# An mLSTM cell and a feed-forward block in float32: where the weights of the third chunk are split, which queue stores them, and when the keys of the next chunk but one are loaded

## The chip, the cores and the metric

The kernel runs on one core of a Trainium2 chip. The metric is device time in microseconds (us). Three runs of the kernel before took 465.68, 472.87 and 473.05 us; their median is 472.87. The engines are named as in the profile: PE (matmul; PEld is its weight load), DVE (vector), ACT (scalar), POOL (GpSimd) and SP, which here only issues DMAs. ACT and POOL can issue DMAs too; what an engine's instruction stream holds is done in order, DMA issues included.

## The reference

The inputs are q, k, v and an output gate of shape (4, 8, 768, 40) (batch B, heads H, sequence S, head size D), an input and a forget gate of shape (4, 8, 768), and two weight matrices, 320x2048 and 2048x320, all float32. First an mLSTM cell runs over the sequence:

```
for t in range(S):
    m_new = maximum(f[t] + m, i[t])
    fs, is_ = exp(f[t] + m - m_new), exp(i[t] - m_new)
    m = m_new
    C = fs * C + is_ * outer(v[t], k[t])
    n = fs * n + is_ * k[t]
    y[t] = sigmoid(o[t]) * (C @ q[t]) / maximum(abs(n . q[t]), 1)
```

Then y, as a matrix x of 3072 tokens by 320, goes through a feed-forward block: h = x @ w_in, g = h * sigmoid(1.702 h), out = g @ w_out.

## The kernel before

**Chunks.** The sequence is cut into NW = 6 chunks of 128 steps, w = 0 to 5; a chunk has 4 x 128 = 512 tokens. In the text, the second, third and fourth chunk are w = 1, 2, 3. The attention of a chunk is computed as small matrix products against the 32 (batch, head) pairs, with a state carried from chunk to chunk. The program is written out by hand: the order of the calls in the source is the order on each engine. One turn of the main loop does the feed-forward block of chunk w and, woven into its second half, the attention of chunk w+1.

**Up stage.** `up_fast(w, j)`, j = 0 to 7, computes h for 256 of the 2048 hidden columns: 16 matmuls of 128x128 by 512 columns (L777). Precision comes from splitting: a weight w_in[n] (n = j // 2, 128x2x512) is rounded to `w_high`, and its rest is kept twice, as `w_low` (w_in - w_high) and, in another scaling, as `w_diff`; the activations are split in the same way into x_high, x_low, x_diff and x_rest. Pass j=0 takes the operands in the order high, rest, low, rest, diff, the others rest, diff, high, low. ACT copies the "side" sums out of PSUM (L801), DVE adds the "main" sums (L805), ACT applies the GELU (L754). The banks in PSUM alternate: pass j+2 needs those of pass j to be read out. In chunk w=1, n = 2 and 3 (`LATE`) are not split yet: L782 uses the unsplit weights there.

**Down stage.** `down_fast` gives 14 products (i = 0 to 13) of g with w_out (L868), each 16 instructions in the trace. After product i, `side[i]` runs parts of the attention of chunk w+1: for w+1 = 2 to 5, scaling and weights at i = 0 to 2, `carry` (p_c, with the keys k_st) at 3, `scores` (p_s) at 4, `values` (p_o, p_i) at 5 and 6, the seam at 6, 10 and 11. The seam brings y into the feed-forward layout: stores to DRAM (`seam_out`, L562), loads back into q_sq (`seam_in`, L571), block transposes on DVE (`seam_turn`), and the splits of x (`split_x`, `split_on`).

**Where the splits live.** `split_high` (L688, ACT), `split_diff` (L691, DVE) and `split_low` (L697, POOL or DVE) make the three parts. The tiles share slots in turn: w_high 2 and 3 go to the slots of w_in 1 and 2, so w_high 3 needs w_in 2 to have been read for the last time, by split_diff and split_low of 2. In chunk w=2, w_low 2 and 3 take the slots of g 2 and g 3 of chunk 1 and w_diff those of its `sums`; g 6 and g 7 of chunk 2 take the slots of w_low 2 and 3 again. w_diff and w_low do not stay in SBUF: `keep` (L701) stores them to DRAM rows (`w_row`, 512 KB each), `fetch_diff` (L725) and `fetch_low` (L721) load them again for each later chunk, in the down stage ahead of it: w_diff 0 and 1 and w_low 2 at i = 11, w_diff 2 and 3 at i = 13. w_low 3 is loaded once by `keep_last` (L705) to stay.

**Loads.** From w=1 on all loads are issued by SP, in this order around the change. In the up stage of chunk w, for the attention of chunk w+1: the gates' round trip through DRAM (m_row, st_row, raw, wt; L310 to L409) and v_st and k_st (L126). At the end of the up stage the output gate `eo` (L128). In the down stage, the gates fi of chunk w+2 (L98), `load_squares(w+2, "k")` (L114: four DMAs of 320 KB into k_sq, which the next up stage turns into kT from its pass j=3 on) at i = 0, the seam's loads, fetch_diff, fetch_low, the stores of `out` (L877), and `load_squares(w+2, "q")` (into q_sq) at i = 13.

The lines that matter most, of the up stage and the down stage in the main loop of the kernel before:

```
                if w == 2 and j == 1:
                    for n in LATE:
                        split_high(n); split_diff(n); split_low(n, G)
                if w == 2 and j == 3:
                    for n in LATE:
                        keep(w_diff_row, n, w_diff[2, n]); keep(w_low_row, n, w_low[2, n])
                    keep_last()
...
            if w and w + 2 < NW and i == 0:
                load_squares(w + 2, "k")
```

Of the kernel before, what the change touches and what calls it, by code (L numbers as in the profile page):

```python
# [8 lines left out]
FP = mybir.dt.float32  # L9
# [22 lines left out]
def kernel(  # L32
# [12 lines left out]
    nc = tc.nc  # L45
# [4 lines left out]
    NW = S // L  # L50
# [25 lines left out]
    V, A, G, T = nc.vector, nc.scalar, nc.gpsimd, nc.tensor  # L76
# [31 lines left out]
    def load_squares(w, what):  # L108
        for dst, src in [((k_sq, k), (q_sq, q))["kq".index(c)] for c in what]:
            x = src[:, :, w * L:(w + 1) * L, :].rearrange("b (p two) (r c) d -> two r (b p) (c d)", two=2, c=4)  # L110
            for i in range(2):
                for n in range(2):
                    r, at = slice(i * 64 + n * 32, i * 64 + n * 32 + 32), (1 - n) * 32
                    nc.sync.dma_start(out=dst[r, at:at + BH // 2 * 4 * D].rearrange("r (j x) -> r j x", x=4 * D), in_=x[i])  # L114

    def load(w, what, bs=slice(0, B)):
        hs = slice(bs.start * H, bs.stop * H)
        for c in what:
            if c == "o" and w not in eo:
                eo[w] = ld.tile([L, BH, D], FP, tag="eo", bufs=1, name="eo")  # L120
            dst, src = {"k": (k_of(w), k), "q": (q_st, q), "v": (v_st, v), "o": (eo.get(w), o_gate)}[c]
            if w and c in "kv":
                for i, t, r in ((0, slice(0, L), slice(0, L)), (1, slice(0, HL), slice(HL, L)),
                                (1, slice(HL, L), slice(0, HL))):
                    x = src[:, :, w * L + t.start:w * L + t.stop, :].rearrange("b (p two) s d -> two s (b p) d", two=2)
                    nc.sync.dma_start(out=dst[r, i::2, 0:D], in_=x[i])  # L126
                continue
            nc.sync.dma_start(out=dst[:, hs, 0:D],  # L128
                              in_=src[bs, :, w * L:(w + 1) * L, :].rearrange("b h s d -> s (b h) d"))
# [538 lines left out]
    w_high, w_low, w_diff, w_rest = {}, {}, {}, []  # L668
    w_low_row, w_diff_row = {}, {}
    LATE = (2, 3)  # L670
# [15 lines left out]
    def split_high(n):  # L686
        w_high[n] = win.tile([128, 2, 512], FR, tag="wb" if n < 2 else "wa", name="w_high")
        A.activation(out=w_high[n], in_=w_in[n], func=AF.Copy, scale=BIAS)  # L688

    def split_diff(n):  # L690
        V.scalar_tensor_tensor(out=w_diff[2 if n in LATE else 1, n], in0=w_high[n], scalar=-1.0 - 1.0 / BASE,  # L691
                               in1=w_in[n], op0=OP.mult, op1=OP.add)

    def split_low(n, engine):
        if n not in LATE:
            w_low[n] = win.tile([128, 2, 512], FR, tag="wa" if n else "wb", name="w_low")
        engine.tensor_tensor(out=w_low[2, n] if n in LATE else w_low[n], in0=w_in[n], in1=w_high[n], op=OP.subtract)  # L697

    def keep(row, n, x):
        row[n] = rows.tile([128, 1024], FP, tag=f"{'d' if row is w_diff_row else 'l'}{n}", bufs=1, name="w_row")  # L700
        nc.sync.dma_start(out=row[n], in_=x.rearrange("p c m -> p (c m)").bitcast(FP))  # L701

    def keep_last():
        w_low[3] = work.tile([128, 2, 512], FR, tag="wx", bufs=1, name="w_low")
# [10 lines left out]
    def split_rest_low():  # L715
        wr = w_rest[0]
        V.tensor_tensor(out=wr[64:128, 0::2], in0=w_in_x[0:64], in1=wr[0:64, 0::2], op=OP.subtract)
        V.tensor_tensor(out=wr[64:128, 1::2], in0=w_in_x[64:128], in1=wr[64:128, 1::2], op=OP.subtract)
# [169 lines left out]
    def run(calls):  # L888
        for f, *args in calls:
            f(*args)  # L890
# [62 lines left out]
    for w in range(NW):  # L953
        more = w + 1 < NW
        if w == 0:
            for j in range(NF // 2):
                if j % 2 == 0:
                    ahead, behind = converted[j // 2]
                    run([(convert, p) for p in ahead] + [(fetch, p) for p in fetched.get(j // 2, ())])
                    up(w, j, lambda: run([(columns_turn, 1) if p is None else (convert, p) for p in behind]))  # L960
                if j == 6:
                    load(1, "o")
                if j == 1:
                    wait_for(w_in[1][:, 1, :])
                    scale(0, 1)
                    load(1, "v")
                if j < B and j % 2:
                    carry(0, j // 2)
                if j == 3:
                    masks()  # L970
                    gates(1)
                    columns_in(1)
                if j == 4:
                    spread(1)
                    load_squares(1, "q")
                if j >= B:
                    transposes(1, j - B)
        else:
            if w == 1:
                split_diff(1)  # L980
                split_low(1, V)
            for j in range(NF // 2):
                up_fast(w, j)
                if more and j == 0:
                    gates(w + 1)
                    if w == 1:
                        wait_for(ends[w + 1])
                if w == 1 and j < 4:
                    weight_sums(j)
                if w == 1 and j == 1:  # L990
                    for n in (0, 1):
                        keep(w_diff_row, n, w_diff[1, n])
                if w == 2 and j == 1:
                    for n in LATE:
                        split_high(n)
                        split_diff(n)
                        split_low(n, G)
                if w == 2 and j == 3:
                    for n in LATE:
                        keep(w_diff_row, n, w_diff[2, n])  # L1000
                        keep(w_low_row, n, w_low[2, n])
                    keep_last()
                if more and j == 2:
                    columns_in(w + 1)
                    spread(w + 1)
                    load(w + 1, "vk")
                if more and j:
                    for n in ((), (), (0, 2), (4, 6), (1, 3), (5, 7), ())[j - 1]:
                        block_transposes(w + 1, n)
                if more and j == 7:  # L1010
                    columns_turn(w + 1)
                lag = 3 if w == 1 else 2
                if lag <= j < 4 + lag:
                    hidden_difference(w, j - lag)
                if j >= 6:
                    hidden_sums(w, (j - 6,), G)
            gelu_fast(w, NF // 2 - 1, 1)
            if more:
                load(w + 1, "o")
            hidden_sums(w, (2, 3), V)  # L1020
        side = attention(w + 1) if more else {}
        if more:
            rooms(w + 1)
        if w == 0:

            blocks = [(lambda b=b, n=n: down(w, b, n)) for n0 in (0, 2) for b in range(B) for n in (n0, n0 + 1)]
        else:
            blocks = down_fast(w, 0) + down_fast(w, 1)
        for i, block in enumerate(blocks):
            if w == 0 and i in (0, 4, 5):  # L1030
                convert((17, 18, 19)[max(i - 3, 0)])
                if i == 0:
                    for n in (1, 3, 5, 7):
                        block_transposes(1, n)
            if w + 2 < NW and i == (6 if w == 0 else 0):
                load_gates(w + 2)
            if w and w + 2 < NW and i == 0:
                load_squares(w + 2, "k")
            if w == 0 and i == 13:
                load_squares(w + 2, "k")  # L1040
            if w == 0 and i == 15:
                load_squares(w + 2, "q")
            block()
            run(side.get(i, []))
            if w == 0 and i == 5:
                split_high(0)
                split_rest()
                split_high(1)
            if w == 0 and i == 9:
                split_diff(0)  # L1050
                split_low(0, V)
                split_rest_low()
            if w and more:
                if i == 11:
                    fetch_diff(w + 1, (0, 1))
                    if w > 1:
                        fetch_low(w + 1)
                if i == 13:
                    if w > 1:
                        fetch_diff(w + 1, (2, 3))  # L1060
                    if w + 2 < NW:
                        load_squares(w + 2, "q")
# [30 lines left out]
```

## Time and profile before

| | |
|---|---|
| median of three runs | 472.87 us |
| the profiled execution | 470.54 us |
| its span, first to last instruction | 468.8 us |
| mean granted PE clock in the span | 0.988 |
| PE / PEld busy | 452.9 us (97%) / 394.8 us (84%) |
| DVE / ACT / POOL busy | 330.2 (70%) / 213.2 (45%) / 134.6 us (29%) |
| DMA | 65.43 MB, mean 140 GB/s |
| up stages of w = 1, 2, 3, 4, 5 | 30.89, 37.59, 29.40, 29.41, 29.39 us |
| down stages of w = 1, 2, 3, 4, 5 | 42.98, 41.20, 41.90, 39.25, 30.44 us |

The stages are read from the chain that ended last: the up stage from the first p_h product (L777) of a chunk to its first p_out product (L868), the down stage from there to the next chunk's first p_h. The last down stage holds no attention. The work of the up stages of w = 2 to 5 is the same on PE, and so is that of the down stages of w = 1 to 3; the one of w = 4 leaves out one half of `carry`.

How to read the rows: a row of the chain or the timeline begins with the start and the length in us; then come the engine, the program's tile and the source line, and xN counts the instructions. A name with q (SPq, ACTq) is that engine's issuing of DMAs. A row of waits names who waited, for whom, the total, how often, and the longest.

### The profile page before, as it was taken

How to read it: one execution, taken by the hardware profiler on the slowest of the kernel's cores; microseconds unless marked ns; L12 is line 12 of the kernel's file. 1: busy time of each engine (PE TensorE's matmuls, PEld its weight loads, DVE VectorE, ACT ScalarE, POOL GpSimd, SP SyncE). 2: the span in 40 equal slices, each digit the busy share in tenths (PEclk: the TensorE clock that was granted, in tenths of full speed). 3: DMA queues.
4: the chain of work that ended last, by engine and by line, in shares of the span. 5: the costliest groups of instructions: out<-in, count | busy, mean ns of one | idle time of the engine just before them, and what ended most of it. 6: DMA issues, size and time to landing. Idle time of an engine off the chain costs nothing.

```text
span 468.8 us, 12126 instructions
## 1 busy us (share of the span) xinstructions
PE 452.9 (97%) x4967; PEld 394.8 (84%) x4967; DVE 330.2 (70%) x663; ACT 213.2 (45%) x470; POOL 134.6 (29%) x126
## 2 busy tenths in 40 slices
PE   9999999999999899978899999989999999999997
PEld 6877877776889899856899988979988999988996
DVE  5788999699769777654767788667778767743512
ACT  5686779403748301563830175920175930276100
POOL 5101318000677600092630035520025530035000
PEclk9999999999999899989899999999999999999999
DMA  9999999049999426769934697943694904610000
GB/s 173 203 301 209 247 202 185 3 105 201 200 154 154 71 60 185 147 125 259 184 57 101 204 206 142 171 84 83 206 224 97 167 20 107 214 73 0 1 28 29
DMA packets 139015, 65.43 MB, mean 140 GB/s; under 512 B 102368, under 2 KB 132016, under 8 KB 138960
## 3 DMA queue, kind: packets, MB, share of 16 engines
q1 hardware_dynamic: 130592, 62.85, 63.4%
q10 hardware_dynamic: 8048, 1.66, 1.7%
q8 instruction: 39, 0.64, 0.6%
q0 software_dynamic: 320, 0.15, 0.2%
q14 instruction: 16, 0.13, 0.1%
HBM read 53.95 MB, written 10.68 MB: 138 GB/s over the span
## 4 chain that ended last, share of the span: by engine, by line
PE 85%; DVE 4%; SPq 3%; DMA 2%; issue 2%; ACT 1%; POOL 1%; ACTq 0%; DVEq 0%; POOLq 0%
PE p_out L868 34%; PE p_h L777 23%; PE p_h L632 6%; PE p_out L814 4%; PE p_h L782 3%; PE p_c L608 2%; PE p_s L465 2%; SPq L126 2%; PE p_o L509 2%; PE p_i L517 2%; PE p_h L641 2%; PE p_t L392 1%; PE p_s L454 1%; DMA w_row<-w_low 1%; DMA k_sq<-in_k_dram 1%
## 5 line engine op out<-in xcount | busy, mean ns | idle before, releaser
L805 DVE SCALAR_TENSOR_TENSOR g<-p_h,g 128x512 f32<-128x512 f32 x80 | 52.8, 687 | 46.2 <-ACT g L801 20.7
L868 PE MATMUL p_out<-w_out_sb,g 128*128 128x160 f32 x480 | 70.7, 305 | 3.7 <-ACT g L801 3.7
L868 PEld LDWEIGHTS p_out<-w_out_sb,g 128*128 128x128 f32 x480 | 68.0, 194 | 4.6 <-ACT g L801 4.1
L801 ACT ACTIVATE g<-p_h 128x512 f32<-128x512 f32 x80 | 46.6, 590 | 42.3 <-PE p_h L777 34.8
L754 ACT ACTIVATE g<-g 128x512 f32<-128x512 f32 x80 | 50.1, 628 | 32.6 <-DVE g L805 32.5
L736 ACT ACTIVATE x_high<-xT 128x512 fp32r<-128x512 f32 x10 | 6.3, 631 | 122.5 <-DVE xT L578 122.5
L836 POOL TENSOR_TENSOR g<-g 128x512 f32<-128x512 f32 x20 | 25.5, 1289 | 121.1 <-ACT g L754 121.1
L873 DVE TENSOR_TENSOR o_sb<-o_sb,p_out 128x160 f32<-128x160 f32 x70 | 21.0, 318 | 46.2 <-PE p_out L868 46.1
L777 PE MATMUL p_h<-x_rest,w_rest 128*128 128x512 f32 x160 | 50.6, 402 | 2.7 <-ACT g L801 2.7
L868 PE MATMUL p_out<-t_sb,s 128*128 128x160 f32 x320 | 47.2, 301 | 0.3 <-DVE state L585 0.3
L868 PEld LDWEIGHTS p_out<-t_sb,s 128*128 128x128 f32 x320 | 44.4, 190 | 0.6 <-DVE state L585 0.5
L777 PE MATMUL p_h<-x_high,w_high 128*128 128x512 f32 x144 | 44.8, 398 | 0.1
L777 PE MATMUL p_h<-x_diff,w_diff 128*128 128x512 f32 x144 | 44.8, 398 | 0.0
L777 PE MATMUL p_h<-x_low,w_low 128*128 128x512 f32 x144 | 44.2, 393 | 0.6 <-DVE x_low L746 0.6
L441 ACT ACTIVATE wt<-wt,cols 128x64 f32<-128x64 f32 x160 | 38.8, 333 | 0.1
L777 PEld LDWEIGHTS p_h<-x_rest,w_rest 128*128 128x128 f32 x160 | 30.1, 189 | 10.0 <-ACT g L801 3.1
L814 PE MATMUL p_out<-w_out_sb,g 128*128 128x320 f32 x128 | 35.7, 436 | 0.0
L777 PEld LDWEIGHTS p_h<-x_low,w_low 128*128 128x128 f32 x144 | 27.3, 190 | 6.8 <-DVE x_low L746 1.0
L777 PEld LDWEIGHTS p_h<-x_diff,w_diff 128*128 128x128 f32 x144 | 27.4, 190 | 6.3
L777 PEld LDWEIGHTS p_h<-x_high,w_high 128*128 128x128 f32 x144 | 27.2, 191 | 6.3 <-ACT x_high L736 0.6
L814 PEld LDWEIGHTS p_out<-w_out_sb,g 128*128 128x128 f32 x128 | 24.0, 190 | 9.5
L632 PE MATMUL p_h<-xT,w_in 128*128 128x256 f32 x128 | 29.6, 385 | 0.0
(191 smaller groups left out, 796.5 us busy)
## 6 DMA issues: line engine op xcount, KB each, us to landing
w_diff<-w_row SPq DMA_DIRECT2D x14, 512.0 KB, 4.4
q_sq<-in_q_dram SPq DMA_DIRECT2D x20, 320.0 KB, 8.8
wt<-m_row SPq DMA_DIRECT2D x20, 256.0 KB, 5.5
k_sq<-in_k_dram SPq DMA_DIRECT2D x16, 320.0 KB, 6.5
bits<-in_moe_w_in_dram SPq DMA_DIRECT2D x8, 512.0 KB, 9.4
out_dram<-o_sb SPq DMA_DIRECT2D x24, 160.0 KB, 1.9
eo<-in_o_gate_dram SPq DMA_DIRECT2D x5, 640.0 KB, 6.6
bits<-in_moe_w_out_dram SPq DMA_DIRECT2D x8, 320.0 KB, 5.6
```

The lines of the kernel that those rows point to most:

```text
L126: nc.sync.dma_start(out=dst[r, i::2, 0:D], in_=x[i])
L441: A.activation(out=x[:, h, :], in_=x[:, h, :], func=AF.Exp, scale=-1.0, bias=cols[w][:, c * PH + h:c * PH + h + 1])
L632: T.matmul(ph[j][i][:, t], w_in[f // 4][:, c, f % 4 * 128:f % 4 * 128 + 128], x[:, c, t], start=(first and c == 0 and n == 0), stop=(not f ...
L754: A.activation(out=g, in_=g, func=AF.Gelu_apprx_sigmoid)
L777: T.matmul(dst[i], a(i), x, start=(k == 0), stop=(k == (1 if whole else 3)))
L782: T.matmul(main[i][:, c * W // 2:(c + 1) * W // 2], w_in[n][:, k, col(i)], xT[w, c][:, k].rearrange("p b t -> p (b t)"), start=(k == 0 and ...
L801: A.activation(out=g[:, i, :], in_=side[i], func=AF.Copy, scale=-BASE)
L805: V.scalar_tensor_tensor(out=g[:, i, :], in0=main[i], scalar=1.0 if whole else 1.0 + 1.0 / BASE, in1=g[:, i, :], op0=OP.mult, op1=OP.add)
L814: T.matmul(po, gs[w, f // 2][:, f % 2, b * L:(b + 1) * L], w_out_sb[:, f, :], start=(f == 0), stop=(f == NF - 1))
L836: G.tensor_tensor(out=a10, in0=a00, in1=a10, op=OP.subtract)
L868: T.matmul(po, a(f), b[:, f, :], start=(f == 0), stop=(f == NH - 1))
L873: V.tensor_tensor(out=dst, in0=x, in1=po, op=OP.add)
```

## The change

In the down stage of w=1 and at the head of the up stage of w=2, the splits of the weights n = 2 and 3 are made which were made after its pass j=1: w_high 2 after product 5 of w=1; w_diff 2, w_low 2, w_high 3 and w_low 3 ahead of pass 0 of w=2; w_diff 3 after pass 0 and the gates. `keep` issues its stores from ACT's queue (`nc.scalar`) instead of SP's, also those of w_diff 0 and 1 in w=1; the stores of n = 2 and n = 3 are issued after passes 0 and 1 (`keep_late`) instead of after pass 3. `keep_last` stays on SP after pass 3. The key loads of `load_squares(w + 2, "k")` for w = 1, 2, 3 go from before product 0 to after product 6 and its part of the attention, which on SP is after the seam's last loads and before fetch_diff. (In chunk w=0 nothing moves.)

```diff
     def keep(row, n, x):
...
-        nc.sync.dma_start(out=row[n], in_=x.rearrange("p c m -> p (c m)").bitcast(FP))
+        nc.scalar.dma_start(out=row[n], in_=x.rearrange("p c m -> p (c m)").bitcast(FP))
+
+    def keep_late(n):
+        keep(w_diff_row, n, w_diff[2, n])
+        keep(w_low_row, n, w_low[2, n])
...
+            if w == 2:
+                split_diff(2)
+                split_low(2, G)
+                split_high(3)
+                split_low(3, G)
             for j in range(NF // 2):
                 up_fast(w, j)
...
-                if w == 2 and j == 1:
-                    for n in LATE:
-                        split_high(n)
-                        split_diff(n)
-                        split_low(n, G)
+                if w == 2 and j < 2:
+                    keep_late(2 + j)
+                if w == 2 and j == 0:
+                    split_diff(3)
                 if w == 2 and j == 3:
-                    for n in LATE:
-                        keep(w_diff_row, n, w_diff[2, n])
-                        keep(w_low_row, n, w_low[2, n])
                     keep_last()
...
-            if w and w + 2 < NW and i == 0:
-                load_squares(w + 2, "k")
...
+            if w == 1 and i == 5:
+                split_high(2)
+            if w and w + 2 < NW and i == 6:
+                load_squares(w + 2, "k")
```

## The prediction

> **What bounds the kernel now.** The profiled execution took 470.54 us, 468.8 of them the span; the median of the three runs shown is 472.87. I read the shares first (PE 97% busy), so only time in which PE stands still or runs slowly is to be had. Then the chain that ended last, in order of time (start, length, what):
>
> ```profile
> 186.74 3.71 PE p_h L777 x16
> ...
> 198.13 3.39 POOL w_low L697
> 201.54 1.06 ACT w_high L688
> ...
> 205.49 0.59 SPq L126
> ...
> 216.11 0.60 SPq L701
> 216.82 4.28 DMA w_row<-w_low
> 221.17 0.60 ACT g L801
> ...
> 223.68 0.61 ACT g L801
> 224.33 10.64 PE p_out L868 x64
> ...
> 336.83 29.41 PE p_h L777 x128
> 366.24 8.69 PE p_out L868 x64
> ```
>
> The third chunk (w=2) is the sick one: its up stage takes 186.74 to 224.33 = 37.59 us and its first 64 products 10.64, where w=4 needs 29.41 and 8.69 for the same instructions. That is 10.13 us too many. In it the chain leaves PE for the weight split (POOL, ACT) and then for SP, whose stores wait behind the v and k loads (L126).
>
> The list of waits of PE after 112 us (engine, line, what ended the wait: total, times, longest):
>
> ```profile
> PE p_out L868 <- ACT g L801: 3.7, 1, 3.7
> PE p_s L465 <- issue: 3.4, 2, 1.8
> PE p_h L777 <- ACT g L801: 2.7, 1, 2.7
> ```
>
> Two waits of 2.68 and 3.66 are the third chunk's. After each, PE is slow: 16 matmuls after the first take 5.35 us for 3.67 (+1.68), 64 after the second 10.64 for 8.69 (+1.95). The four make 9.97. The "issue" row is another stall, in the score matmuls of the second and the fourth chunk; the chain shows the first:
>
> ```profile
> 156.83 0.97 PE p_s L465 x56
> 157.81 1.85 issue
> 159.65 1.43 PE p_s L465 x72
> 161.08 3.87 PE p_out L868 x16
> ```
>
> Scores take 4.25 us for 2.02 elsewhere, and the next 16 products 3.87 for 2.37. Products and attention together take 42.98 us in w=1 (143.76 to 186.74) and 41.90 in w=3 (294.93 to 336.83), against 39.25 in w=4: 3.73 and 2.65 lost. Looked at in half microseconds, the DMA view shows what PE waited for: one 16 KB packet of the instruction queue at 156.5, and one at 308.5, in the very slices in which the k_sq loads run dry; in w=2 at 237.0 (k_sq dry, too), in w=4, which has no k_sq load, at 375.5, when the o load runs dry. PE goes on some 3 us after that packet. The fetch came out only when the data was through.
>
> **The change, part by part.**
>
> **Splits.** Same instructions, other places. w_high 2 (1.04 us on ACT) goes into w=1's product 5, where ACT is idle from 156.2 to 175.1. w_low 2 (POOL, 3.39) may start when the slot it takes from gs[1,2] is read out, after product 10 at 180.1 (171.33 + 4 x 2.2), and ends by 183.5; POOL is idle from 160.0 to 198.1. w_diff 2 (DVE, 1.23) goes behind the last o_sb add, 188.7 to 190.0, inside DVE's idle 2.43 before 191.16. w_high 3 is an added wait at the head of ACT's up stage: it needs w_in 2 read out by POOL and DVE, so 190.0 to 191.0. Behind it stand the evacuations of j=0, which slip from 190.5 to 191.1; PE wants their banks for j=2 at 194.1. w_low 3 runs on POOL to 194.5 (behind it hidden differences, first wanted after j=2), w_diff 3 on DVE behind the gates, 196.3 to 197.5. What is late next is j=1: its sums on DVE end at 198.8 instead of 197.0, then on ACT two stores (to 200.0) and the evacuations of j=2, to 201.6; PE wants those banks for j=4 at 201.4. So the wait of 2.68 and its slow clock go, but for 0.2, which I leave out.
>
> **Stores.** Four of w_diff/w_low (and two of w=1) move from SP to ACT's queue, 0.4 to 1.1 us of issue each. On ACT they sit behind the GELU of j=0 and j=1, where the splits that they wait for are done by the times above; behind them are the evacuations just counted, and ACT has 2.1 us of such work per 3.67 of a pass. They land 4.3 to 4.8 us after issue, by about 199 and 205, instead of 221.1 and 223.6; g 6 no longer waits. g 7 still takes w_low 3's slot, which PE reads to the end of j=7, so the first product waits for one evacuation: 0.6 to 0.7. **Sum: 9.97 - 0.7 = 9.3 us off.** If ACT's cover is gone, up to 4 x 0.7 = 2.8 returns.
>
> **Keys.** The four k_sq loads (L114) of w=1, 2, 3 go from before the products to behind the second seam (product 6's list). SP then issues them right after the last seam load and *ahead of* the w_diff loads. (a) The fetches no longer stand behind them: 3.73 + 2.65 = **6.4 off**, as w=4. Bounds: nothing (the stall has another cause) and 6.4. (b) The SP queue keeps its order in landing: an 8 KB m_row store issued behind the q_sq loads needs 8.4 us. So w_diff, needed at once, waits for 1.3 MB of keys. SP and PE in time order, at the start of the third chunk:
>
> ```profile
> 148.92 1.95 SPq L114 DMA_DIRECT2D k_sq<-in_k_dram  x4
> ...
> 179.93 1.23 SPq L571 DMA_DIRECT2D q_sq<-x_rest  x2
> 181.46 1.30 SPq L725 DMA_DIRECT2D w_diff<-w_row  x2
> ```
> ```profile
> 189.36 1.07 PE L777 MATMUL p_h<-x_diff,w_diff 128*128 128x512 f32 x4
> ```
>
> From the first k_sq issue (148.92) the queue is dry at 156.75: 7.85 us. The first w_diff then needs 1.5 of transfer (two of them land 1.6 apart) and 0.9 to be reported: 10.25 after SP reaches the keys. SP reaches them at 181.2, 260.7 and 331.35 (the end of the last seam load's issue); PE wants w_diff 0 after 12 of 16 matmuls, its weights a little before: 2.65 after the up stages begin (186.74, 265.53, 336.83), at 189.4, 268.2, 339.5. Late by 2.15, 2.75, 2.1: **7.0 on**. Bounds: nothing, if w_diff overtakes the keys (alone it lands in 3.5 to 4.0), and some 4.9 each if the last key load needs 9.1 us, as the slowest q_sq load did. Each wait of that size has a slow clock behind it: 1.5 after 1.85 us, 1.68 after 2.68, 1.95 after 3.66, nothing after the 1.58 in w=3. I take 1.7 x 3 = **5.1 on** (bounds 0 and 5.9). Nothing hides it: j=0 runs in program order.
>
> After the 1.85 us wait the granted clock reads 0.67 and then 0.50 in the two stretches of 2 us from 160. [...]
>
> The instruction packets above come when the data queue is dry, four times in four. [...]
>
> (c) Later loads. q_sq, m_row and the v, k loads follow the keys on SP and slip by 3 to 5 us, PE by 3.8 to 4.5; k_st landed some 0.8 us before its first use in w=4, so 0 to 1 there; I take nothing. In w=2 the o load now ends about 230 while the scores begin at 231.6; in w=2 of before that distance was 2.2 us and there was no stall, in w=1 none was left. Bounds 0 and 3.7; I take 0.
>
> **Sum:** -9.3 - 6.4 + 7.0 + 5.1 = -3.6; 470.5 - 3.6 = **466.9 us**, 1.3% under the median, 0.8% under the profiled execution. About 2% (9.5 us) is what a measurement of this kernel can tell from no change: the runs alone go from 465.68 to 473.05.
>
> **Rivals.**
> *The keys are through in time* (w_diff under 0.5 us late): for it, the queue moves 400 GB/s in some stretches, and 2 us late out of 10 is a fine balance; against it, k_sq moved at 200 GB/s with nothing beside it (150 to 156). Then only -9.3 - 6.4 = -15.7: 454.8.
> *The fetch stalls come back*, since w=2's o load ends later or fetches meet other loads: +3.7 to +6.4, that is 470.6 to 473.3.
> *The third chunk stays sick*, the change not doing what it says: ACT's waits for POOL's w_low stand ahead of evacuations. Against it POOL's 38 us of idleness. The 9.3 are not had: 476.2.
> *Slower than before:* late w_diff, doubled. Place: the eighth of up stage j=0 that uses w_diff, three chunks. If the key loads land as slowly as the slowest q_sq, w_diff is 4.9 us late, 6.9 with the slow clock, and k_st in w=4 then some 2 late: 3 x 6.9 + 2 = 22.7 on, 15.7 off, 477.5; with a slow clock twice as long in each chunk 483. It decides from 5.2 us per chunk, stall and clock together.
>
> **How the numbers follow.** Forecast (462 to 470) 0.50; keys in time 0.25; fetch stalls 0.12; third chunk sick 0.05; slower 0.08. Range: up to 0.2 left out, from the in-time case to the fetch stalls and the sick chunk's near end: 454 to 474. Faster by over 2% (under 463.4): all 0.25 of in-time and a fifth of the forecast, 0.35; slower by over 2% (over 482.3): about half of the last, 0.05; within: 0.60.
>
> **What would show it.** Right: no wait for w_row or w_high in the third chunk, its up stage 29.4 plus the w_diff wait; "issue" gone from PE's waits; a new row "PE p_h L781 <- DMA w_diff<-w_row", about 2 to 3 us three times, and a clock of 0.5 after it in w=2, 3, 4 but not in w=5. Wrong: no such row (in time), or p_s still waiting for issue.

## The result, and the profile after

The changed kernel has a median of 466.27 us (464.30 to 468.47, 20 runs), beside 470.50 us (465.54 to 475.38, 20 runs) for the kernel before on the same chip: a ratio of 0.994, with a 95% interval of 0.9912 to 0.9968. (Here and below, ratios leave out executions over 1.5% above the fastest of the same kernel; medians and ranges hold them all.) The gain is real and small, some 4 us. The profiled execution took 467.89 us, 466.2 of it the span (before: 470.54 and 468.8), with a mean granted clock of 0.987.

So small a difference is a difference of large terms. The first view to read is the list of PE's waits after 112 us of the changed kernel (who waited, for whom: total, times, longest, in us):

```profile
PE p_h L781 <- DMA w_diff<-w_row: 8.1, 3, 3.0
PE p_out L872 <- ACT g L805: 0.7, 1, 0.7
PE p_h L781 <- DVE x_low L750: 0.5, 1, 0.5
```

The two ACT waits of the third chunk and the "issue" row have gone. In their place stands one new row, for the loads of w_diff, three times. The chain that ended last shows each of the three (start, length, what):

```profile
176.50 0.59 SPq L114
...
178.78 8.68 DMA w_diff<-w_row
...
187.51 28.47 PE p_h L781 x116
...
216.65 8.96 PE p_out L872 x64
...
227.62 2.37 PE p_out L872 x16
229.99 2.15 PE p_s L465 x128
232.15 2.37 PE p_out L872 x16
...
253.84 8.19 DMA w_diff<-w_row
...
262.07 28.50 PE p_h L781 x116
...
326.65 8.53 DMA w_diff<-w_row
...
335.23 28.39 PE p_h L781 x116
```

SP issues the keys (L114) at 176.50 and w_diff 2.3 us later, and w_diff then needs 8.2 to 8.7 us. The page's table of DMA issues says it of all fourteen such loads (KB each, median us from issue to landing; before it was 4.4):

```profile
w_diff<-w_row SPq DMA_DIRECT2D x14, 512.0 KB, 8.4
```

What follows each wait is slow, too: 116 matmuls take 28.39 to 28.50 us where 29.40 for 128 would make it 26.64. The windows of 2 us around the first wait show why (stretch, length, busy time and instructions of PE, PEld, DVE, ACT and POOL, then the granted clock, the DMA share and GB/s):

```profile
186.00:188.00 2.00, 0.49 (x2) 0.45 (x3) 0.00 (x0) 0.81 (x1) 1.12 (x1) 1.00 1.01 396
188.00:190.00 2.00, 2.00 (x7) 1.55 (x6) 0.38 (x1) 1.01 (x2) 1.25 (x1) 0.57 1.15 292
190.00:192.00 2.00, 2.00 (x7) 1.56 (x6) 1.93 (x5) 1.97 (x4) 0.00 (x0) 0.58 1.21 188
```

The clock is 1.00 in the stretch of the wait and 0.57 and 0.58 in the two behind it.

By stages, from the first product of one kind to the first of the next, both profiled executions stand against each other so (us):

| stage | before | after | difference |
|---|---|---|---|
| all up to the down stage of w=1 | | | -0.77 |
| down w=1 | 42.87 | 39.15 | -3.72 |
| up w=2 | 37.86 | 34.67 | -3.19 |
| down w=2 | 40.93 | 39.39 | -1.54 |
| up w=3 | 29.51 | 34.37 | +4.86 |
| down w=3 | 41.79 | 39.15 | -2.64 |
| up w=4 | 29.52 | 33.89 | +4.37 |
| down w=4, up w=5 | 68.64 | 68.64 | 0 |

The differences add up to -2.6, as the two spans do. Won are 6.36 in the down stages of w=1 and w=3 and 4.73 in the third chunk, with its own late w_diff in it; 9.23 of that is paid back in the up stages of w=3 and w=4.

### The profile page after: what moved, and what is told of

Its sections match the earlier page's. It is cut to its first block, busy times and chain, and to the rows that moved or that the text cites. A ratio compares the mean times of both kernels' runs of the same rounds, so it can differ in the third digit from the quotient of the medians.

```text
span 466.2 us, 12134 instructions
## 1 busy us (share of the span) xinstructions
PE 450.9 (97%) x4967; PEld 391.9 (84%) x4967; DVE 327.5 (70%) x663; ACT 214.1 (46%) x470; POOL 131.0 (28%) x126
## 4 chain that ended last, share of the span: by engine, by line
PE 53%; DMA 7%; SPq 1%; issue 0%; ACTq 0%; ACT 0%; DVE 0%
PE p_h L781 25%; PE p_out L872 24%; DMA w_diff<-w_row 5%; PE p_o L509 1%; PE p_s L465 1%; PE p_c L608 1%; PE p_i L517 1%; DMA x_row<-y 1%; SPq L114 1%; DMA x_rest<-y 1%; SPq L571 1%; ACTq L562 0%; ACT g L805 0%; DVE o_sb L877 0%; DVE o_sb L875 0%
## 5 line engine op out<-in xcount | busy, mean ns | idle before, releaser
L872 PE MATMUL p_out<-w_out_sb,g 128*128 128x160 f32 x480 | 69.0, 300 | 0.7 <-ACT g L805 0.7
L872 PEld LDWEIGHTS p_out<-w_out_sb,g 128*128 128x128 f32 x480 | 66.3, 190 | 1.6 <-ACT g L805 1.1
L781 PE MATMUL p_h<-x_diff,w_diff 128*128 128x512 f32 x144 | 47.5, 418 | 8.1 <-DMA w_diff<-w_row 8.1
L781 PE MATMUL p_h<-x_rest,w_rest 128*128 128x512 f32 x160 | 52.0, 411 | 0.0
L781 PEld LDWEIGHTS p_h<-x_diff,w_diff 128*128 128x128 f32 x144 | 28.7, 201 | 16.0 <-DMA w_diff<-w_row 9.4
L781 PEld LDWEIGHTS p_h<-x_rest,w_rest 128*128 128x128 f32 x160 | 31.1, 195 | 7.4 <-DVE x_rest L753 0.4
L818 PEld LDWEIGHTS p_out<-w_out_sb,g 128*128 128x128 f32 x128 | 23.9, 190 | 9.6
```

The costliest lines, as they stand in the source:

```text
L781: T.matmul(dst[i], a(i), x, start=(k == 0), stop=(k == (1 if whole else 3)))
L818: T.matmul(po, gs[w, f // 2][:, f % 2, b * L:(b + 1) * L], w_out_sb[:, f, :], start=(f == 0), stop=(f == NF - 1))
L872: T.matmul(po, a(f), b[:, f, :], start=(f == 0), stop=(f == NH - 1))
```

## The experiments

The theory: three separate terms, the splits (about 9 won), the fetch stalls (6.4 won) and the late w_diff with its slow clock (12 lost). The rival: the key loads can be had in time, by their order or by another queue, and then all that is lost comes back, to about 455. A second rival: the stores' new queue is part of the gain. Ratios below are against the kernel before, run beside the variant on the same chip, with 95% intervals; waits are PE's after 112 us, each list of one profiled execution. Comments in the diffs are added here.

### The keys alone

```diff
(before)
-            if w and w + 2 < NW and i == 0:
-                load_squares(w + 2, "k")
...
+            if w and w + 2 < NW and i == 6:
+                load_squares(w + 2, "k")
```

> The kernel before with the key loads moved, and nothing else. Theory (the prices add up: the keys ahead of w_diff cost a wait of 2.2 to 3 us and 1.7 of slow clock at the head of the up stages of w=2, 3 and 4, and give back 6.4 in the fetch stalls): the third chunk stays as it was, 470.5 - 6.4 + 13.4 = 477.5 us, 1.5% slower than before. Rival (the key move is a gain by itself, and only together with the new place of the splits do the loads collide): 464 us.

Measured: 476.65 us (472.94 to 481.36, 10 runs), ratio 1.0125 [1.0084, 1.0166]. The waits, of the one profiled execution, which was the longest of the ten:

```profile
PE p_h L777 <- DMA w_diff<-w_row: 10.3, 3, 4.0
PE p_out L868 <- ACT g L801: 6.3, 1, 6.3
```

No "issue" row: the fetch stalls are gone and w_diff is late, with no split touched. The third chunk stays sick: the stores of L701, still on SP, are issued at 215.8 us as before (216.1), and the first p_out product waits 6.3 us instead of 3.66. That growth is shown for this execution alone. Moved alone, the keys make the kernel slower, by about what the expectation added up.

### The splits and stores alone

```diff
(after)
+            if w and w + 2 < NW and i == 0:
+                load_squares(w + 2, "k")
...
-            if w and w + 2 < NW and i == 6:
-                load_squares(w + 2, "k")
```

> The change without the move of the keys (early splits, stores from ACT's queue). Theory: 470.5 - 9.3 = 461 us; no wait for w_diff in any up stage, a wait of 0.7 at the first product of w=2, and PE still waits for issue in the scores of w=1 and w=3, or in w=2, where the queue now runs dry at another time. Rival (the third chunk was freed by the emptier SP queue, not by the places of splits and stores): 466 us or more, with a wait for w_row or w_high in w=2.

Measured: 467.38 us (464.11 to 471.15, 10 runs), ratio 0.9919 [0.9881, 0.9957]: a miss by 6 us. The waits, and the first stall in the chain (the profiled execution took 471.11; one of the ten was longer, by 0.04):

```profile
PE p_s L465 <- issue: 2.8, 1, 2.8
PE p_o L509 <- issue: 2.5, 1, 2.5
PE p_i L517 <- issue: 2.3, 1, 2.3
PE p_h L781 <- DVE g L809: 1.2, 1, 1.2
PE p_out L872 <- ACT g L805: 0.7, 1, 0.7
```
```profile
160.96 0.72 PE p_o L509 x38
161.67 2.45 issue
164.13 0.60 PE p_o L509 x23
164.73 0.93 PE p_i L517 x64
165.66 4.05 PE p_out L872 x16
```

The third chunk is healed as forecast: no wait for w_row or w_high, its up stage 31.56 instead of 37.59. But the fetch stalls grew. Before had two, in w=1 and w=3; here there are three, one of them in w=2, and each has a slow clock behind it (4.05 us for 16 matmuls that take 2.37, at the first). The down stages of w=1, 2 and 3 take 43.64, 43.91 and 45.19 in this trace, where w=4 takes 39.25: 15.0 lost. So what the early keys cost isn't a fixed 6.4. With a third chunk that comes on time it was 15.0 in this execution, which lies 3.7 above the median. For the median some 11 is an estimate: 6.4, and 4.5 more, since the third chunk won 7.7 here and the median fell by only 3.2. That it depends on where PE stands when the fetch comes out fits both traces, but no run shows it by itself.

The "DVE g" row is new as well: in pass 3 of the third chunk, PE waits 1.2 us for the sums of pass 1, which w_diff 3's split had made late. The prediction had put 0.2 there and left it out. In the changed kernel it does not appear, since PE has already lost more at w_diff.

### The stores back on SP

```diff
(after)
-        nc.scalar.dma_start(out=row[n], in_=x.rearrange("p c m -> p (c m)").bitcast(FP))
+        nc.sync.dma_start(out=row[n], in_=x.rearrange("p c m -> p (c m)").bitcast(FP))
```

> The whole change, but the stores to w_row are issued by SP again, at the new places. Theory (what frees g 6 in the third chunk is that the stores stand ahead of the v and k loads, not which engine issues them): within 1 us of the changed kernel, 465.3 to 467.3. Rival (the ACT queue is what does it): g 6 waits for w_row again, 470 us.

Measured: 466.85 us (464.78 to 468.51, 10 runs), ratio 0.9915 [0.9879, 0.9950], beside 0.994 for the change. No difference: what heals the third chunk is that the splits and stores come earlier. ScalarE's queue has no part in it.

### The keys behind all of the w_diff loads

```diff
(after)
-            if w and w + 2 < NW and i == 6:
-                load_squares(w + 2, "k")
...
                         fetch_low(w + 1)    # i == 11, after fetch_diff 0 and 1
+                    if w + 2 < NW:
+                        load_squares(w + 2, "k")
```

> The whole change, but the four key loads are issued behind fetch_diff 0, 1 and fetch_low (after product 11) instead of ahead of them. Theory (what is lost is the order on SP's queue): no wait for w_diff, no slow clock, no fetch stall: 466.3 - 13.5 = 453 us, plus up to 1.2 where k_st comes late in w=4, so 453 to 455. Rival (w_diff is late because its own slots come free late, or because the queue carries the keys at all): 463 us or more.

Measured: 471.77 us (468.24 to 475.67, 10 runs), ratio 1.0025 [0.9983, 1.0066]. A miss by 17 us, and the most telling one. w_diff is in time, as wanted. But the waits now have

```profile
PE p_c L608 <- DMA k_st<-in_k_dram: 8.7, 2, 6.0
```

and the chain, in the down stages of w=2 and w=3,

```profile
222.98 5.50 DMA k_st<-in_k_dram
...
228.62 3.65 PE p_c L608 x128
...
296.62 5.69 DMA k_st<-in_k_dram
...
302.45 3.44 PE p_c L608 x128
```

The keys k_st of the current attention, the last large load of the up stage, are late, and `carry` runs at a slow clock behind them (3.65 us for 2.01). Without the wait for w_diff, PE reached `carry` of w=2 at 222.7 us (225.6 in the changed kernel), but k_st landed at 228.5 (some 224.0). SP's own waits between 176 and 232 us show what held it:

```profile
SPq L310 <- DMA w_row<-w_diff: 6.7, 1, 6.7
SPq L114 <- DMA w_row<-w_diff: 5.2, 1, 5.2
```

SP waits 5.2 and 6.7 us for stores of w_diff to land before it issues q_sq and the m_row round trip (m_row at 202.01 us; in the changed kernel at 192.08). Neither DMA reads or writes what those stores move. In the trace's records of this stretch, the DMAs of SP and ACT signal on eight semaphores between them, and each of the two waits for the one that it signals itself, which a store of w_diff had used before it; the changed kernel's trace has one such wait, too, of 4.4 us (L313). So SP's order of issue is a second chain beside PE's. In the changed kernel it is hidden: PE, held up by w_diff, comes to `carry` some 1.6 us after k_st has landed.

### Other shares of the keys ahead of w_diff

```diff
(after, three ahead)
-    def load_squares(w, what):
+    def load_squares(w, what, part=(0, 1, 2, 3)):
...
+                    if i * 2 + n not in part:
+                        continue
...
-                load_squares(w + 2, "k")
+                load_squares(w + 2, "k", (0, 1, 2))     # i == 6; two ahead: (0, 1)
...
+                    if w + 2 < NW:                      # i == 11, after fetch_low
+                        load_squares(w + 2, "k", (3,))  # two ahead: (2, 3)
```

> The changed kernel with three of the four key loads ahead of fetch_diff and the fourth behind fetch_low. A key load takes 1.64 us of the queue. Theory: the wait for w_diff shrinks from 2.7 to 1.1 us in each of the three chunks, too short for a slow clock behind it (none followed the 1.58 us in the kernel before): 8.1 + 5.4 become 3.2 + 0 at that place, and what of it k_st takes back is seen at carry; 458 to 465 us. Rival (every wait at this place brings the slow clock): 1.7 us remain behind each, 463 to 466 us.

> As e8, but two key loads ahead of fetch_diff and two behind fetch_low. Theory (a key load more or less ahead of w_diff shifts it by 1.64 us; the queue's total does not change, and what PE does not wait for w_diff it waits for k_st, v_st or the state): no wait for w_diff; waits at carry between those of e8 (3.4) and e3 (8.7): 462 to 468 us. Rival (the fewer ahead the better): under 460 us.

Measured: three ahead 462.44 us (460.59 to 464.90, 4 runs), ratio 0.9796 [0.9755, 0.9837]; two ahead 464.36 us (461.87 to 468.25, 5 runs), ratio 0.9849 [0.9780, 0.9919]. Both times are as the theory had it. The waits with three ahead (the lines of these kernels lie two further down):

```profile
PE p_h L783 <- DMA w_diff<-w_row: 2.6, 2, 1.5
PE p_out L874 <- DVE state L587: 2.3, 1, 2.3
PE p_h L783 <- DVE g L811: 1.2, 1, 1.2
```

The 2.3 of the second row are put down to DVE, but most likely aren't its doing (see two early, two late, below). With two ahead w_diff is in time and k_st late three times (4.8 us together), and there is a stall of 2.5 us at `carry` of w=3 ("issue"). By the number of key loads ahead of w_diff, the ratio goes 4: 0.994, 3: 0.980, 2: 0.985, 0: 1.0025. The better shares lie where neither of two loads is very late; the intervals of 3 and 2 overlap, so which of these is better isn't shown.

Three ahead shows one thing more. Behind its wait of 1.53 us at 257 us the clock does not fall (windows, columns as above):

```profile
257.00:259.00 2.00, 0.47 (x3) 0.39 (x3) 0.00 (x0) 0.00 (x0) 0.00 (x0) 1.00 1.02 408
259.00:261.00 2.00, 2.00 (x11) 1.62 (x10) 0.52 (x1) 1.13 (x3) 0.00 (x0) 1.00 1.09 305
```

Where it is so, a w_diff that is 1 us less late saves nearly 3, an estimate from the changed kernel's numbers: the 1 us of wait, and the 1.8 of slow clock (1.75 to 1.86 there). But three ahead isn't free of it: behind the 2.3 us at 298.7 the clock reads 0.51 and 0.64 in the stretches from 300 and 302.

### Loads issued by ScalarE

```diff
(after: keys from ScalarE)
-    def load_squares(w, what):
+    def load_squares(w, what, queue=nc.sync):
...
-                    nc.sync.dma_start(...)
+                    queue.dma_start(...)
...
-                load_squares(w + 2, "k")
+                load_squares(w + 2, "k", nc.scalar)
(keys and q from ScalarE: also, at i == 13)
+                        load_squares(w + 2, "q", nc.scalar)
(q from ScalarE: the q line alone, with the keys behind the w_diff loads)
```

> The changed kernel, but its key loads (after product 6, ahead of fetch_diff) are issued by ACT. [...] Rival (w_diff waits for the keys whichever queue they are on): wait for w_diff of 2 to 3 us three times as in the changed kernel, 466 us.

> The changed kernel, with the key loads after product 6 and the q_sq loads after product 13 both issued by ACT. Theory: neither w_diff nor the gates' round trip stands behind 1.3 MB of its own queue; no wait for w_diff, little for k_st: 455 to 460 us. Rival (engines full): a wait for w_diff or k_st of 2 us or more per chunk, 464 us or more.

> As e3 (keys behind fetch_diff and fetch_low), and the four q_sq loads after product 13 are issued by ACT instead of SP, on a queue of its own. In e3 PE waited 8.7 us for k_st at carry: SP's queue lands in order, and the gates' round trip (m_row, st_row), and after it raw, wt, v_st and k_st, stood behind keys and q_sq. Theory (the order on SP's queue is what makes them late): with q_sq on the other queue the round trip is through 3 to 5 us sooner, k_st comes in time or nearly so, 456 to 461 us. Rival (the DMA engines are simply full there, and it is all one by which queue a load comes): PE waits for k_st as in e3, 466 us or more.

Measured: keys 467.42 us (466.16 to 468.76, 5 runs), ratio 0.9910 [0.9881, 0.9939]; keys and q 468.61 us (466.74 to 470.72, 10 runs), 0.9921 [0.9890, 0.9952]; q 468.50 us (465.38 to 473.13, 10 runs), 0.9939 [0.9900, 0.9978]. The first is inside the 464 to 468 us that were forecast for it, but not for the reason forecast, a late k_st; the other two are misses. With the keys on ScalarE's queue PE waits for neither w_diff nor k_st. It waits for ACT instead (a wait, and ACT's timeline at the seam before w=2):

```profile
PE p_h L781 <- ACT x_high L740: 5.1, 3, 2.7
```
```profile
174.37 5.96 ACTq L114 DMA_DIRECT2D k_sq<-in_k_dram  x4
180.43 0.63 ACT L740 ACTIVATE x_high<-xT 128x512 fp32r<-128x512 f32 x1 [22.70 <-DVE s L857]
...
185.69 0.63 ACT L740 ACTIVATE x_high<-xT 128x512 fp32r<-128x512 f32 x1 [4.32 <-DVE xT L578]
```

ACT stands 5.96 us in the issue of four loads (SP took 2.18 for the same four in the changed kernel), but that isn't what PE waits for. Its 2.7 us end with the second x_high, at 186.3, and this stood 4.32 us behind the transposes xT, which waited for the seam's loads into q_sq. SP issues the last of these from 176.4 us on, when ACT has been sending keys since 174.4; the seam's loads of w=2 take 3.0 to 7.5 us to land, against 2.2 to 3.4 in the changed kernel, where SP issues them ahead of the keys. In w=3 and w=4, too, the second x_high waits for xT. And w_diff needs 6.0 us in the median (before 4.4, in the changed kernel 8.4). So a queue of its own does not keep the keys from delaying other loads. With keys and q both there, the wait for x_high is 6.4 in all. With q alone, ACT's evacuations are late (3.3), and w_diff again (5.3, in its later loads); why the latter isn't settled.

### Two keys early, two late

```diff
(after, with the parts as above)
+            if w and w + 2 < NW and i == 0:
+                load_squares(w + 2, "k", (0, 1))
...
-            if w and w + 2 < NW and i == 6:
-                load_squares(w + 2, "k")
...
+                    if w + 2 < NW:                      # i == 11, after fetch_low
+                        load_squares(w + 2, "k", (2, 3))
```

Two loads go back to the place they had before. The data queue then runs dry earlier than with all four there (at 157.5 us in w=1, where it was 161.5 with the splits alone), and SP has less to issue at the seam.

> Of the four key loads two are issued ahead of product 0, as all four were before the change, and two behind fetch_low. A look at the fetch stalls alone. Theory (an instruction packet comes out only when the data queue is dry, and PE goes on some 3 us later): two key loads keep the queue busy 3.3 us longer than in the changed kernel, to 156.5 in w=1, 231 in w=2 and 300.5 in w=3, where the scores begin at about 155, 230 and 303.6: PE waits for issue in w=1 and w=2, not in w=3, and the packets lie in the slices in which the queue runs dry. [...]

> The kernel of e11 again, timed. Its one execution took 458.42 us. Theory (two key loads fit ahead of the dense groups, the other two behind w_diff leave the rest of SP's queue early enough): under 462 us, below the changed kernel and below three ahead (462.4). Rival (a lucky execution; some executions meet the fetch stalls of 2 to 4 us): a median of 462 to 466 us, with a wide spread.

Measured: 458.42 us in the first, single execution, then 457.98 us (457.19 to 461.49, 6 runs), ratio 0.9735 [0.9685, 0.9786]. This is faster than both kernels. Its waits and its row of the granted clock (40 slices of the span, 9 is full):

```profile
PE p_out L874 <- DVE state_mid L619: 1.9, 1, 1.9
PE p_h L783 <- DVE g L811: 1.2, 1, 1.2
PE p_out L874 <- ACT g L807: 0.7, 1, 0.7
PE p_h L783 <- DVE x_low L752: 0.5, 1, 0.5
```
```profile
PEclk9999999999999999999999999999999999999999
```

No wait for a load, no "issue" row, and a clock that never falls. But the largest wait is not DVE's. The chain has it in w=3:

```profile
294.57 0.50 DVE state_mid L619
295.07 0.62 issue
295.69 2.44 PE p_out L874 x16
```

PE goes on 0.62 us after that sum is done, and by the changed kernel it doesn't need that sum: there the same product starts at 301.27, when of these sums on DVE only the first `state_mid` is through (300.98) and the second hasn't begun (302.04); here the first is through at 293.51. What fits is a fetch: a 16 KB packet of the instruction queue comes at 292.8 us, as the data queue runs dry, and PE goes on 2.9 us later, as after the other packets. With three ahead the 2.3 us in w=3 look the same (first `state_mid` through at 296.1, packet at 295.9, PE on at 298.72). So two early and two late has most likely a fetch stall left, of 1.9 us.

The count of stalls was a miss: waits for a fetch were expected in w=1 and w=2 and not in w=3. The first execution's list has one, of 0.7 us, in w=2, and 1.0 us put down to `state` in w=3, 3.0 us after a packet at 292.5. In its w=1, one instruction packet got through at 153.8 us, between the o load and the keys, and the next at 157.8, when the keys were through; PE hadn't yet run out.

### w_diff 3 split one pass later

```diff
(three ahead)
-                if w == 2 and j < 2:
-                    keep_late(2 + j)
-                if w == 2 and j == 0:
+                if w == 2 and j in (0, 2):
+                    keep_late(2 + j // 2)
+                if w == 2 and j == 1:
                     split_diff(3)
```

> As e8 (three key loads ahead of fetch_diff, the fourth behind fetch_low); besides, w_diff 3 is split after pass 1 of w=2 instead of after pass 0, and the stores of n=3 go after pass 2. In e8 PE waits 1.2 us in pass 3 of w=2 for the sums of pass 1, which stand behind this split on DVE. Theory: that wait goes and nothing takes its place, since g 7 is written 15 us later: 1.2 us less than e8, 460 to 462 us. Rival (DVE is late there anyway, by the gates): the wait stays.

Measured: 463.09 us (460.22 to 465.81, 6 runs), ratio 0.9820 [0.9763, 0.9877], beside 0.9796 for three ahead. The "DVE g" wait of 1.2 is gone from the trace, so w_diff 3's split was its cause. The time shows nothing of it: 460 to 462 was expected. The waits put down to `state` and `state_mid` in the down stages are 3.7 together (3.2 with three ahead), and the larger, of 2.5, again ends 2.9 us after an instruction packet (296.1, 299.01). Whether the 1.2 was lost there or just lies within the spread of 5 us stays open.

## Why the prediction was right, and where it was not

The forecast was 466.9 us; the median is 466.27, the profiled execution 467.89. The sum of -3.6 stands against -2.6 between the two profiled executions. That the median lies so close is in part luck: the four terms below come to -1.8, another -0.8 was won ahead of the first stage that they are about, and the profiled execution lies 1.6 above the median of its twenty. Term by term:

**Splits, -9.3.** Right. The third chunk went down by 4.73 with 4.33 of late w_diff and slow clock in it (2.50 + 1.83): 9.06. The 0.6 to 0.7 for g 7's slot is there as 0.7. Two details fell. The 0.2 that was left out is 1.2 wherever w_diff doesn't cover it, so the splits alone are worth less: the up stage of w=2 and the 64 products behind it win 7.7 in the splits-only trace. And the stores' queue, which the prediction priced with the rest, plays no part.

**Fetch stalls, -6.4.** Right in the pair of profiles: -3.72 and -2.64 for 3.73 and 2.65. As a statement of what early keys cost it was wrong: "as w=4" holds for the down stage without keys, but the cost with keys isn't a property of the keys. It was 6.4 in the one schedule and 15.0 in one execution of the other. The bound of 0 to 3.7 for w=2 was the place to see it: with the splits alone, where that chunk comes on time, it has a stall of 2.3, and before, where it was late, none. Around the dense groups of matmuls the rows on the packets held. In the changed kernel they come at 153.4, 228.3 and 297.8 us, the first as the data queue runs dry and the others some half a microsecond after, and no stall follows; in w=2 the scores begin 1.7 us after the packet, at 229.99. But "when the data queue is dry", as the prediction read it from four packets, does not hold for every packet. Elsewhere in the changed kernel's trace 16 KB packets of the instruction queue come out in the midst of data: at 168.7, 192.2 and 220.4 us, with 416, 156 and 456 packets of the data queue in the same half microsecond. What makes a packet wait in the one place and not in the other, no run shows.

**Late w_diff, +7.0.** The mechanism, the place and the number of times are right; the size was 8.1 (2.50, 2.99, 2.65 for 2.15, 2.75, 2.1). The mis-sized term is the time from SP's first key issue to w_diff: 10.25 was worked out, and it took 10.5 to 11.0. (By the prediction's own times the first wait comes to 2.05, not 2.15; and a q_sq load of 9.6 us stands in w=4 of before, above the 9.1 of its bound.) w_diff lands behind the keys in all three places. The rival in which w_diff overtakes was wrong.

**Slow clock, +5.1.** Measured 1.83 + 1.86 + 1.75 = 5.4. The waits of w=2, 3 and 4 have it, the start of w=5 doesn't. But "each wait of that size" was too strong: with the stores back on SP, w=2 waits 1.96 us for w_diff, and the granted clock behind it reads 1.00 in both stretches of 2 us.

**Later loads, nothing.** Right as a number for the change, and the step that misleads most. The nothing is cover: the wait for w_diff hides the lateness of k_st. With w_diff on time and the keys right behind it, k_st costs 8.7 us of waits, and the kernel is where it was. The rival "keys in time, 454.8" left this out: it took two terms of the sum away and let the rest stand. None of the three places tried for the four loads as one block reaches it (467.38, 466.27, 471.77), nor does another queue as tried here; shares of the keys, two early and two late, come to 457.98.

What remains open: why a packet of instructions waits for the data in some places; how far the 1.9, 1.2 and 0.7 us that are left in the best kernel can still be won; and how much of the spread of single runs, 5 to 8 us in many of these kernels and 4.3 in the best, is stalls that come in some executions and not in others.

## What to carry to other kernels

A load that is moved in a queue's order does not only free its old place: name what it now stands in front of, and then what is late next once that is mended, for a wait on the critical path covers others behind it (here the 8.1 us for w_diff covered a wait for k_st that came to 8.7 without them). A large load that fits nowhere whole may fit in parts; here halves at two places did what neither place could do for the whole. A wait that comes with a slow clock should be priced as both (in the changed kernel 2.50 to 2.99 us and 1.75 to 1.86 more), so shortening it until the clock stays up is worth more than its own length. And the name beside a wait is to be checked: where the named work was done well before, or another trace shows that it isn't needed, something else was awaited.

## What the runs showed of the hardware

- **The clock fell after some short waits.** The waits of 1.85, 2.50, 2.65, 2.68, 2.71, 2.99 and 3.66 us in these traces have a stretch of granted clock near 0.5 to 0.9 behind them, worth 1.5 to 1.95 us each in the kernels before and after; so have all others of 2.27 us and more after 112 us in the runs here. The waits of 1.1, 1.5 and 1.58 us don't, and neither do 1.84 (keys and q from ScalarE, at 261.8 us), 1.88 (two early, timed) and 1.96 (stores back on SP), where the clock reads 1.00 on both sides. So the length alone doesn't decide between 1.85 and 1.96; what does, no run tells.
- **PE stood still where the profile names nothing to wait for.** In the kernel before (packets at 156.5 and 308.5 us), with the splits alone (161.5, 237.0 and 307.0) and in the first execution of two early (230.5), 16 KB packets of the instruction queue came out around dense groups of small matmuls when SP's data queue had run dry or was about to, and PE went on some 2 to 3 us after the packet, having stood still for 0.7 to 2.8 us ("issue"). That PE lacked instructions there is an inference from these times. Packets at other places came in the midst of data, and without a stall (192.2 us in the changed kernel). A stall that looks the same stands in the list of two early, timed, under DVE's name (1.9 us).
- **Loads delayed each other within a queue and across queues.** w_diff needed 4.4 us in the median with no keys ahead of it (before), 8.4 behind four key loads in its own queue (the changed kernel) and 6.0 beside them on the other queue (keys from ScalarE); the seam's loads went from 3.4 to 7.5 at the longest when keys of the other queue were ahead of them.
- **Issuing took time on the engine that issues.** Four loads of 320 KB held ACT for 5.96 us (keys from ScalarE) and SP for 2.18 (the changed kernel), and SP waited up to 6.7 us at an issue for a store with which it shares no data (the keys behind all of the w_diff loads).
